# States and scores of a unit in one TensorE block, and where the scores' banks come from

## The chip, the cores and the metric

The kernel runs on one core of one Trainium2 chip. The metric is device time in microseconds (us) of one execution; the reference point is the median of three runs. A core has five engines that work side by side and wait for each other by semaphores: PE (TensorE, matrix products), DVE (VectorE), ACT (ScalarE), POOL (GpSimd) and SP (SyncE, which here only starts transfers). Matrix products write to PSUM, eight banks of 2 KB for each of 128 partitions; VectorE and ScalarE read them from there.

## What is computed

A gated linear recurrence over 768 positions for 4 x 8 heads of width 48, and an MLP with an ELU between its two products on all 3072 tokens:

```python
f = 1.0 / (1.0 + np.exp(-f_logit))
for t in range(S):
    state = f[:, :, t, :, None] * state + np.einsum('bhd,bhe->bhde', k[:, :, t], v[:, :, t])
    y[:, :, t] = np.einsum('bhd,bhde->bhe', q[:, :, t], state)
x = y.transpose(0, 2, 1, 3).reshape(B * S, H * D)          # 3072 x 384
h = x @ w_in                                               # 384 -> 2048
g = np.where(h > 0.0, h, np.exp(np.minimum(h, 0.0)) - 1.0)
out = g @ w_out                                            # 2048 -> 384
```

The weights arrive as 64-bit floats and are unpacked to 32-bit on the chip.

## The kernel before

**Units.** The tokens are cut into 12 units of 256 (u = 0 to 11, three to a sequence, four chunks of 64 in a unit). For a unit the attention part computes, for all 8 heads in 4 pairs: the transposed keys (`transposed`, L669), the products of keys and values that move the state from chunk to chunk (`advance`, L728, tile psU, 64 small matmul records in two banks), the running states (`step`, L686 to L691, one addition a chunk on VectorE; the first of a sequence is a ScalarE copy, L688, the last chunk of a unit that isn't the end of a sequence has a multiplication more, and the last chunk of a sequence has none), the scores within chunks (`scores`, L705, tile psS, 64 records in two banks), the causal mask on them (`mask`, L713, two VectorE instructions, tile at), and then the outputs from the masked scores (`outputs`, L743) and from the states (`carried`, L763, whose results ScalarE copies to xt at L770 and L772, with two transfers after it). The small products use quarters of the array, 64 by 64.

**The MLP** runs one unit behind. It goes in 8 parts P of a unit: `up` (L927 for the first unit, `up7` with L882 for the others, which form the product by seven smaller ones and sums) makes a part of h in tile psH, `joined` (L904) adds the pieces, `exped` (L914, L915) applies the exponential on ScalarE, `elu` (L936) finishes it, POOL forms sums of it (L946), and `down` (L981; L959 for the first unit) accumulates the part into psM, four banks m0 to m3 (m1 and m2 alone for the first unit). After the eighth part `down` has the four banks added and stored (L991, L992). A `down` runs LAG = 2 parts after its `up`.

**Banks.** PSUM's eight banks are two for psH, m0 to m3 for psM, and a0 and a1, which psT, psU, psS and psY of the attention use in turn. A tile that takes a bank waits until the readers of the tile before it are done.

**Order.** The order on each engine is written out by hand: a loop over steps T, 16 to a unit (P = T // 2), with a plan of what else is issued at a step:

```python
if T % 2 and sevens:
    joined(P)
if T % 2 == 0 and P and order[P - 1][0] < DIRECT:
    elu(P - 1)
for f in plan.pop(T, ()):
    f()
if T % 2 == 0:
    up(P)
elif P >= LAG:
    down(P - LAG)
```

An even step ends with an up block and an odd one with a down block on TensorE. The tuples A1, A2 and A3 say at which steps, counted from the unit's first, `attention` issues transposed, advance, step, scores with mask, outputs and carried: for u = 1 at 2, 5, 6, 8, 10, 11, and for u from 3 on at 2, 4, 5, 7, 9, 11 (T in this text is counted from the unit's first step; up(2) is the up block of T=4, "down block 0" the first of the unit whose MLP runs, at T=5). At the steps of u = 1 the weights are still being unpacked: `merge(n)` at step n on VectorE (L581), `split` and `lower` (L563, L567, L573) two steps ahead. There `watch(1)` at step 3 lowers the flag column `fine` (L650) where decays have grown too large. From unit 4 on VectorE also checks the range of the weights again at every fourth step (L603). `warm` (L1036) issues matmuls whose result nobody reads.

Of the kernel before, what the change touches and what calls it, by code (L numbers as in the profile page):

```python
# [356 lines left out]
def fast(ctx: ExitStack, tc: tile.TileContext, q, k, v, f_logit, w_in, w_out, out, flag, outer):  # L357
# [18 lines left out]
    nc = tc.nc  # L376
# [7 lines left out]
    NC = U // C  # L384
    UPB = S // U
    NU = B * UPB
    HP = H // 2
    NFT = DFF // 128
# [5 lines left out]
    LAG = 2  # L394
    AHEAD = 7
    WA = 1
    F1 = (1, 3)
    W0 = 3
    HOLD = 2
    A1 = (2, 5, 6, 8, 10, 11)  # L400
    D2 = (16, 18, 20, 22)
    A2 = (23, 25, 25, 26, 27, 28)
    D3 = (-7, -5, -3, -1)
    A3 = (2, 4, 5, 7, 9, 11)
    BL = 13
    RR = 0
    MX = 10
# [254 lines left out]
    def transposed(u, h, bank, pairs=(0, 1)):  # L662

        if 0 in pairs:
            pts[u, h] = ps.tile([128, 2, NW, 128], FP32, tag=bank, name=f"psT{u}_{h}")
            kns[u, h] = sb.tile([128, 2, NW, 128], FP32, tag="kn", name=f"kn{u}_{h}")
        for p in pairs:
            for w in range(NW):
                nc.tensor.transpose(  # L669
                    pts[u, h][:, p, w], in_=qkf[u % NB]["k"][:, 2 * h + p, w * W : (w + 1) * W], identity=ident[:]  # L670
                )
        p = slice(pairs[0], pairs[-1] + 1)
        nc.scalar.copy(kns[u, h][:, p], pts[u, h][:, p])
# [3 lines left out]
    def step(u, c):  # L677

        if u % UPB == UPB - 1 and c == NC - 1:
            return  # L680
        new = pus[u][c % 2][:, c // 2]
        box = boxes[(u * NC + c) % len(boxes)]
        s = box[:].rearrange("n (p d) -> n p d", d=64)[:, 0:HP, PAD:]
        if u % UPB or c:
            old = sts[u, c][:].rearrange("n (p d) -> n p d", d=64)[:, 0:HP, PAD:]
            nc.vector.tensor_tensor(out=s, in0=new, in1=old, op=ALU.add)  # L686
        else:
            nc.scalar.copy(s, new)  # L688
        if c == NC - 1:
            end = qkf[u % NB]["f"][:, :, 1, U - 1 :].broadcast_to([128, HP, D])  # L690
            nc.vector.tensor_tensor(out=s, in0=s, in1=end, op=ALU.mult)  # L691
        sts[(u, c + 1) if c < NC - 1 else (u + 1, 0)] = box

    def scores(u, banks=("a0", "a1"), pairs=range(HP), pc=None):

        t = qkf[u % NB]
        if pc is None:
            ats[u] = sb.tile([128, 2, NW, HP, C], FP32, tag="at", name=f"at{u}", bufs=1)
            pc = [ps.tile([128, NW, HP, C], FP32, tag=banks[r], name=f"psS{u}_{r}") for r in range(2)]
        for p in pairs:  # L700
            for w in range(NW):
                for b in range(2):
                    cols = slice(w * W + b * C, w * W + b * C + C)
                    for r in range(2):
                        nc.tensor.matmul(  # L705
                            pc[r][FULL[b], w, p], lhsT=t["k"][FULL[r], p, cols], rhs=t["q"][FULL[r], p, cols],
                            start=True, stop=True,
                        )
        return pc

    def mask(u, pc):
        for r in range(2):
            nc.vector.tensor_tensor(  # L713
                out=ats[u][:, r].rearrange("k w p i -> k (w p) i"), in0=pc[r][:].rearrange("k w p i -> k (w p) i"),
                in1=twice[:].unsqueeze(1).broadcast_to([128, NW * HP, C]), op=ALU.mult,
            )

    def advance(u, pairs=range(HP)):

        if u not in pus:  # L720
            pus[u] = [ps.tile([128, NW, HP, D], FP32, tag=n, name=f"psU{u}_{n}") for n in ("a0", "a1")]
        pu = pus[u]
        for p in pairs:
            for w in range(NW):
                for r in range(2):
                    h = 2 * p + r
                    for b in range(2):
                        nc.tensor.matmul(  # L728
                            pu[b][FULL[r], w, p], lhsT=kns[u, p // 2][FULL[b], p % 2, w, FULL[r]],
                            rhs=vs[u % NB][FULL[b], w, PAD + h * D : PAD + (h + 1) * D],  # L730
                            start=(w == 0 and p == 0), stop=(w == NW - 1 and p == HP - 1), skip_group_check=True,
                        )

    def outputs(u, banks=("a0", "a1")):


        pys[u] = [ps.tile([128, NW, HP, C], FP32, tag=banks[b], name=f"psY{u}_{b}") for b in range(2)]
        at = ats.pop(u)
        for w in range(NW):
            for p in range(HP):  # L740
                for r in range(2):
                    for b in range(2):
                        nc.tensor.matmul(  # L743
                            pys[u][b][FULL[r ^ b], w, p], lhsT=of_head(u, b, w, r, p),
                            rhs=at[FULL[b], r, w, p], start=(w == 0 and p == 0), stop=False,
                            skip_group_check=True,
                        )

        for b in range(2):
            nc.scalar.copy(between[:], pys[u][b][:, :, :, 0])  # L750

    def carried(u):

        t = qkf[u % NB]
        py = pys.pop(u)
        for w in range(NW):
            for p in range(HP):
                for b in range(2):
                    c = 2 * w + b
                    if (u % UPB, c) == (0, 0):  # L760
                        continue
                    for r in range(2):
                        nc.tensor.matmul(  # L763
                            py[b][FULL[r ^ b], w, p], lhsT=sts[u, c][FULL[r], 64 * p + r * PAD : 64 * (p + 1) + r * PAD],
                            rhs=t["q"][FULL[r], p, c * C : (c + 1) * C],
                            start=False, stop=True, skip_group_check=True,
                        )
        x = xts[u] = sb.tile([128, HP + 1, U], FP32, tag="xt", name=f"xt{u}", bufs=3)
        to = x[:, 0:HP].rearrange("n p (w b i) -> n b w p i", b=2, i=C)
        nc.scalar.copy(to[:, 0], py[0][:])  # L770
        for r in range(2):
            nc.scalar.copy(to[FULL[r], 1], py[1][FULL[1 - r]])  # L772
        for r in range(2):
            frm = PAD + D * r
            (nc.sync if u > 1 else nc.scalar).dma_start(
                out=x[GAP[r] : GAP[r] + PAD, 0:NKT], in_=x[frm : frm + D, NKT]
            )
# [46 lines left out]
    def at_step(step, *todo):  # L824
        plan.setdefault(step, []).extend(todo)

    def attention(u, first, then):

        kept = []
        for p, i in enumerate(first):  # L830
            at_step(i, (lambda: settle(u)) if p == NKT else lambda p=p: decays(u, p))
        if u > 1:
            at_step(then[0], lambda: transposed(u, 0, "a0"), lambda: transposed(u, 1, "a1"))
        at_step(then[1], lambda: advance(u))
        at_step(then[2], *(lambda c=c: step(u, c) for c in range(NC)))
        at_step(then[3], lambda: kept.append(scores(u)), lambda: mask(u, kept[0]))
        at_step(then[4], lambda: outputs(u))
        at_step(then[5], lambda: carried(u))

    gs, ss, pms, phs = {}, {}, {}, {}  # L840

# [187 lines left out]
        nc.tensor.matmul(pf[0:1, :], lhsT=low[:], rhs=causal[:, W - 1 : W], start=True, stop=True)  # L1029
        nc.vector.tensor_copy(flag[:], pf[0:1, :])  # L1030

    def warm(n, bank="m0"):

        pw = ps.tile([128, 4, 128], FP32, tag=bank, name="psW")
        for _ in range(n):
            nc.tensor.matmul(  # L1036
                pw[:], lhsT=ident[:], rhs=ident[:].unsqueeze(1).broadcast_to([128, 4, 128]), start=True, stop=True
            )
# [81 lines left out]
    at_step(F1[1], lambda: move(1, 1, nc.scalar), lambda: watch(1))  # L1120
    at_step(F1[1] + 2, lambda: scale(1, ("q", NKT, nc.gpsimd)))
    at_step(A1[0], lambda: transposed(1, 0, "a0"), lambda: transposed(1, 1, "a1"))
    attention(1, (), A1)
    at_step(8, lambda: load(2))
    at_step(14, lambda: gates(2))
# [8 lines left out]
    for u in range(3, NU):  # L1134
        t = (u - 1) * NFT
        at_step(t + BL, lambda u=u: blend(u))
        at_step(t - 16, lambda u=u: load(u))
        at_step(t - 8, lambda u=u: gates(u))
        attention(u, [t + i for i in D3], [t + i for i in A3])
    for n in range(NR):  # L1140
        t = 3 * NFT + (NU - 4) * NFT * n // NR + RR
        at_step(t, lambda n=n: reread(n))
# [3 lines left out]
    for T in range(NU * NFT):  # L1146
        P = T // 2
        sevens = order[P][0] >= DIRECT
# [5 lines that stand above are left out]
            f()  # L1154
        if T % 2 == 0:
            up(P)
        elif P >= LAG:
            down(P - LAG)
        for n in later.pop(T, ()):
            split(n)  # L1160
            lower(n)
# [53 lines left out]
```

## Time and profile before

| | us |
|---|---|
| median of three runs | 567.27 (566.85 to 568.79) |
| span of the profiled execution | 567.3 |
| mean granted TensorE clock | 0.997 |
| one unit of TensorE from u = 3 on | 43.7 to 43.8 |

A line of the timeline gives start and length in us, the engine, the line of the kernel, the operation, what it writes and reads, its shape and how many instructions are merged in it; in square brackets is how long the engine stood idle before it and what ended that. PE is TensorE's matmuls and PEld its weight loads. The length of a merged line reaches to the end of its last instruction, and as matmuls overlap, the distance between starts is the better price. The chain of waits follows the end of the kernel back to what released each step.

### The profile page before, as it was taken

The numbers are of one execution on the slowest core, as the hardware profiler recorded it, in microseconds if no ns is written. First come the engines' busy times: TensorE is split into PE (matmuls) and PEld (weight loads), VectorE is DVE, ScalarE is ACT, GpSimd is POOL, SyncE is SP. The second block draws the span as 40 slices with busy tenths as digits, with TensorE's granted clock in tenths as the row PEclk, the third lists the DMA queues.
The fourth block names the chain that finished last, engine by engine and source line by source line (L and its number), as shares of the span: only waits on it lengthen the run. The fifth ranks groups of instructions, "written<-read, shape, count | busy, mean of one in ns | idle before, by whom it ended". The sixth has DMA issues, their size and how long they took to land.

```text
span 567.3 us, 15527 instructions
## 1 busy us (share of the span) xinstructions
PE 547.5 (97%) x6336; PEld 509.7 (90%) x6336; DVE 409.4 (72%) x802; ACT 230.2 (41%) x424; POOL 292.7 (52%) x567
## 2 busy tenths in 40 slices
PE   6879998999999999999999999999999999999996
PEld 3566677999999999999999999999999999999996
DVE  8779989785675785885785885786776876745543
ACT  3287862443343433434343343333343343233331
POOL 6601788475374465456366357257248348325332
PEclk9899999999999999999999999999999999999999
DMA  8997951024024225215216216206206203201001
GB/s 212 266 261 209 298 129 43 3 47 114 3 46 138 65 52 145 79 42 156 78 36 155 86 38 153 86 19 173 84 14 178 84 6 74 84 2 36 29 2 35
DMA packets 38193, 53.30 MB, mean 94 GB/s; under 512 B 3712, under 2 KB 27936, under 8 KB 38112
## 3 DMA queue, kind: packets, MB, share of 16 engines
q1 hardware_dynamic: 37312, 51.62, 34.2%
q8 instruction: 52, 0.85, 0.7%
q10 hardware_dynamic: 800, 0.59, 0.4%
q14 instruction: 29, 0.24, 0.1%
HBM read 44.04 MB, written 4.72 MB: 86 GB/s over the span
## 4 chain that ended last, share of the span: by engine, by line
PE 81%; DMA 7%; DVE 7%; issue 2%; POOL 1%; ACT 1%; SPq 0%; DVEq 0%; ACTq 0%; POOLq 0%
PE psH L882 36%; PE psM L981 36%; DMA area<-in_moe_w_in_dram 4%; PE psS L705 2%; PE psY L743 2%; PE psY L763 2%; PE psU_a L728 2%; DVE f L631 2%; PE psT L669 1%; DMA xt<-xt 1%; DMA f<-f 1%; DVE f L626 1%; DMA k<-in_k_dram 1%; DVE bits L563 1%; DVE area L850 1%
## 5 line engine op out<-in xcount | busy, mean ns | idle before, releaser
L882 PE MATMUL psH<-xt,wi 128*128 128x128 f32 (+1 forms) x1056 | 195.0, 294 | 0.1
L946 POOL TENSOR_TENSOR sums<-gg 128x128 f32<-128x128 f32 x176 | 77.7, 462 | 214.5 <-DVE gg L936 205.9
L882 PEld LDWEIGHTS psH<-xt,wi 128*128 128x128 f32 x1056 | 149.5, 192 | 1.8 <-DVE hh L891 0.4
L914 ACT ACTIVATE gg<-hh 128x512 f32<-128x512 f32 x88 | 55.5, 631 | 232.0 <-DVE hh L904 154.6
L882 PE MATMUL psH<-xt,area 128*128 128x128 f32 x704 | 121.8, 275 | 1.3 <-DVE hh L904 1.0
L882 PEld LDWEIGHTS psH<-xt,area 128*128 128x128 f32 x704 | 106.5, 191 | 6.3 <-PE psH L882 1.3
L891 DVE TENSOR_TENSOR hh<-psH,u 128x256 f32<-128x256 f32 x88 | 37.1, 422 | 93.9 <-ACT u L889 93.9
L981 PE MATMUL psM<-area,sums 128*128 128x192 f32 x528 | 100.2, 326 | 0.0
L981 PEld LDWEIGHTS psM<-area,sums 128*128 128x128 f32 x528 | 88.2, 190 | 0.0
L981 PE MATMUL psM<-wo,gg 128*128 128x192 f32 x352 | 74.9, 335 | 0.0
L631 DVE RECIPROCAL f<-f 128x256 f32<-128x256 f32 x36 | 62.7, 1747 | 1.1
L936 DVE SCALAR_TENSOR_TENSOR gg<-gg,hh 128x512 f32<-128x512 f32 x88 | 61.9, 703 | 1.5 <-ACT gg L915 1.5
L915 ACT ACTIVATE gg<-gg 128x512 f32<-128x512 f32 x96 | 60.6, 631 | 3.0
L981 PEld LDWEIGHTS psM<-wo,gg 128*128 128x128 f32 x352 | 55.2, 190 | 2.0
L904 DVE TENSOR_TENSOR hh<-psH,u43h 128x256 f32<-128x256 f32 (+1 forms) x176 | 54.7, 352 | 3.0
L946 POOL TENSOR_TENSOR sums<-gg,sums 128x128 f32<-128x128 f32 x88 | 47.0, 534 | 6.9
L889 ACT COPY u<-psH 128x128 f32<-128x128 f32 x88 | 23.1, 263 | 60.9 <-PE psH L882 60.9
L621 POOL TENSOR_TENSOR q<-q,f 128x256 f32<-128x256 f32 x48 | 35.7, 745 | 21.8 <-DVE f L631 10.6
L904 DVE TENSOR_TENSOR u43h<-psH,hh 128x256 f32<-128x256 f32 x88 | 37.1, 422 | 12.7 <-PE psH L882 12.4
L621 POOL TENSOR_TENSOR k<-k,f 128x256 f32<-128x256 f32 x48 | 40.7, 851 | 7.1 <-DMA f<-f 5.1
L981 PE MATMUL psM<-area,gg 128*128 128x192 f32 x176 | 43.0, 326 | 0.0
L981 PE MATMUL psM<-wo,sums 128*128 128x192 f32 x176 | 43.0, 326 | 0.0
(97 smaller groups left out, 672.3 us busy)
## 6 DMA issues: line engine op xcount, KB each, us to landing
area<-in_moe_w_out_dram SPq DMA_DIRECT2D x8, 768.0 KB, 9.6
again<-in_moe_w_in_dram SPq DMA_DIRECT2D x16, 384.0 KB, 4.2
again<-in_moe_w_out_dram SPq DMA_DIRECT2D x16, 384.0 KB, 3.5
k<-in_k_dram SPq DMA_DIRECT2D x12, 384.0 KB, 4.5
q<-in_q_dram SPq DMA_DIRECT2D x12, 384.0 KB, 5.4
v<-in_v_dram SPq DMA_DIRECT2D x12, 384.0 KB, 5.8
area<-in_moe_w_in_dram SPq DMA_DIRECT2D x8, 576.0 KB, 8.4
out_dram<-o SPq DMA_DIRECT2D x42, 96.0 KB, 1.7
```

Source lines behind the costliest of these rows:

```text
L621: e.tensor_tensor(out=t[n][:, p], in0=t[n][:, p], in1=t["f"][:, p, "kq".index(n)], op=ALU.mult)
L631: nc.vector.reciprocal(f[:, p, 1], f[:, p, 0])
L705: nc.tensor.matmul(pc[r][FULL[b], w, p], lhsT=t["k"][FULL[r], p, cols], rhs=t["q"][FULL[r], p, cols], start=True, stop=True,)
L882: nc.tensor.matmul(to, lhsT=lhs, rhs=rhs, start=(n == 0), stop=True, skip_group_check=True)
L889: nc.scalar.copy(u1[:], pa[:, 0])
L891: add = lambda to, x, y: nc.vector.tensor_tensor(out=to, in0=x, in1=y, op=ALU.add)
L904: add = lambda to, x, y: nc.vector.tensor_tensor(out=to, in0=x, in1=y, op=ALU.add)
L914: nc.scalar.activation(g[:], h, AF.Relu, scale=-1.0)
L915: nc.scalar.activation(g[:], g[:], AF.Exp, scale=-1.0)
L936: nc.vector.scalar_tensor_tensor(out=g[:], in0=g[:], scalar=-1.0, in1=phs.pop(P), op0=ALU.add, op1=ALU.max)
L946: nc.gpsimd.tensor_tensor(out=s[:, i], in0=x, in1=y, op=op)
L981: nc.tensor.matmul(pm[bank][:, half * DH : (half + 1) * DH], lhsT=x, rhs=y, start=first, stop=(j == NP - 1), skip_group_check=True,)
```

## The change

A function `both` issues, at one step, the state products in a0 and a1, the scores in m3 and m0, the state additions and the masks. It takes the place of three entries of `attention` where the tuple has four steps instead of six. This holds for u = 1 (steps 2, 6, 8, 10) and for u = 3 to 7 and 9 to 11 (2, 5, 9, 11); u = 2 and u = 8 (`APART`) stay as they were. For the later units the down block of the step with `both` is left out and issued two steps later, ahead of the one that stands there, since m0 and m3 are psM's. For u = 1 the MLP of the first unit uses m1 and m2 alone, and no down block moves. At step 4 of u = 1, 31 matmuls of one column by one column are issued in m3, reading `fine`.

```diff
+    SMALL = 31
-    A1 = (2, 5, 6, 8, 10, 11)
+    A1 = (2, 6, 8, 10)
-    A3 = (2, 4, 5, 7, 9, 11)
+    A3 = (2, 5, 9, 11)
+    APART, B3 = 8, (2, 4, 5, 7, 9, 11)
...
+    def both(u):
+        advance(u)
+        pc = scores(u, ("m3", "m0"))
+        for c in range(NC):
+            step(u, c)
+        mask(u, pc)
...
-        at_step(then[1], lambda: advance(u))
-        at_step(then[2], *(lambda c=c: step(u, c) for c in range(NC)))
-        at_step(then[3], lambda: kept.append(scores(u)), lambda: mask(u, kept[0]))
-        at_step(then[4], lambda: outputs(u))
-        at_step(then[5], lambda: carried(u))
+        if len(then) == 4:
+            at_step(then[1], lambda: both(u))
+        else:
+            at_step(then[1], lambda: advance(u))
+            at_step(then[2], *(lambda c=c: step(u, c) for c in range(NC)))
+            at_step(then[3], lambda: kept.append(scores(u)), lambda: mask(u, kept[0]))
+        at_step(then[-2], lambda: outputs(u))
+        at_step(then[-1], lambda: carried(u))
...
-    def warm(n, bank="m0"):
+    def warm(n, bank="m0", small=0):
         pw = ps.tile([128, 4, 128], FP32, tag=bank, name="psW")
+        for _ in range(small):
+            nc.tensor.matmul(pw[0:1, 0, 0:1], lhsT=fine[:, 0], rhs=fine[:, 0], start=True, stop=True)
...
+    at_step(4, lambda: warm(0, "m3", SMALL))
...
-        attention(u, [t + i for i in D3], [t + i for i in A3])
+        attention(u, [t + i for i in D3], [t + i for i in (B3 if u == APART else A3)])
+    joint = [(u - 1) * NFT + A3[1] for u in range(3, NU) if u != APART]
...
-        elif P >= LAG:
+        elif P >= LAG and T not in joint:
+            if T - 2 in joint:
+                down(P - LAG - 1)
             down(P - LAG)
```

## The prediction

> **What bounds the kernel now.** I read the page first: busy shares, then the chain of waits. TensorE is busy for 97% of the span, and from about 100 us on the chain is nothing but its blocks in turn.
>
> ```profile
> PE 547.5 (97%) x6336; PEld 509.7 (90%) x6336; DVE 409.4 (72%) x802; ACT 230.2 (41%) x424; POOL 292.7 (52%) x567
> ```
>
> So an edit gains only what it takes out of TensorE's own stream, and loses what it makes TensorE wait. I then read the timeline of one unit by engine (the eighth, u = 7; columns are start, length, engine, line, operation, count). TensorE:
>
> ```profile
> 310.50 0.49 PE L981 MATMUL psM<-wo,sums 128*128 128x192 f32 x2
> 310.92 1.15 PE L728 MATMUL psU_a<-v,kn 64*64 64x48 f32 x64
> 312.00 0.49 PE L882 MATMUL psH<-xt,wi 128*128 128x128 f32 x2
> ...
> 314.55 0.82 PE L981 MATMUL psM<-wo,gg 128*128 128x192 f32 x4
> ...
> 319.36 1.16 PE L705 MATMUL psS<-q,k 64*64 64x64 f32 x64
> 320.45 0.92 PE L981 MATMUL psM<-wo,gg 128*128 128x192 f32 x4
> ```
>
> Here T=4 is the state block (310.92) and the up block, 314.55 is the first down block of the new unit (T=5), 319.36 the scores (T=7). Starts give the prices. An up block is 2.44 us and a down block 2.28 where neither touches attention (chain of waits). An attention block of 64 records takes 1.09 (319.36 to 320.45), 17 ns a record; around it the last matmul before and the first ones after are stretched by 0.09 and 0.10, so it costs 1.28. Now VectorE in the same unit:
>
> ```profile
> 311.46 0.36 DVE L991 TENSOR_TENSOR o<-psM,u 128x192 f32<-128x192 f32 x1 [1.62 <-ACT u L992]
> ...
> 315.56 0.42 DVE L904 TENSOR_TENSOR u43h<-psH,hh 128x256 f32<-128x256 f32 x1
> 316.01 0.62 DVE L904 TENSOR_TENSOR hh<-psH,u43h 128x256 f32<-128x256 f32 x2
> 316.55 1.52 DVE L686 TENSOR_TENSOR state<-psU_a,state 128x192 f32<-128x192 f32 x4
> 318.11 0.36 DVE L691 TENSOR_TENSOR state<-state,f 128x192 f32<-128x192 f32 x1
> ...
> 320.57 1.29 DVE L713 TENSOR_TENSOR at<-psS,twice 128x512 f32<-128x512 f32 x2
> ```
>
> The reader is to see that VectorE is on average free but here is not: from 311.46 (output additions of the unit before) to the end of the state additions at 318.39 it never idles. The state block was done near 312.1 and its additions start at 316.55, over 4 us later; the kernel before hides that because the masks (320.57) come two steps later and nobody waits for them until T=9. In units that begin a sequence it is later still (u = 9):
>
> ```profile
> 405.42 0.30 ACT L688 COPY state<-psU_a 128x192 f32<-128x192 f32 x1
> ```
>
> That copy stands behind the activations of T=5 on ScalarE, and VectorE idles 1.63 us for it until 405.75. Last, the start, where the weights are unpacked:
>
> ```profile
> 38.69 2.83 PE L927 MATMUL psH<-xt,wi 128*128 128x256 f32 x12 [2.30 <-DVE wi L581]
> ```
> ```profile
> 42.18 0.10 DVE L650 SCALAR_TENSOR_TENSOR fine<-f,fine 128x3 f32<-128x3 f32 x1
> ```
> ```profile
> 550.16 0.19 PE L1029 MATMUL psF<-causal,low 128*1 128x1 f32 x2
> ```
>
> TensorE starts up(2) (T=4) at 38.69; the flag column `fine` is written at 42.18 by T=3's work, as VectorE is behind; and a one-column matmul's two records start 0.19 - 0.164 = 0.026 us apart.
>
> **What the Trainium skill says.** "TensorEngine Tiling (Array Packing)", Key Properties: changing the tiling mode drains the array. The trace agrees: 0.19 us per 64x64 block. "TensorE: Matmul & The Clock Gate", table at the head: VectorE is a strict first-in first-out queue, and Part 3: matmuls start in program order. The trace agrees (every block in the order of the program), so a mask can't pass the state additions, and no later matmul can pass a waiting one. Same page, Part 1: the array falls to half clock after an idle window of some 3.4 us. Before, 2.30 us of idling at 36.4 to 38.69 left the granted clock at 1.00; the opening matmuls of 512 columns took 0.82 to 0.86 us each cold against 0.46 later.
>
> **The change, part by part.**
>
> *Merging the two blocks, units 3 to 7 and 9 to 11.* 64 + 64 records are the same; one entry and one exit go: -0.19 us in each of 8 units, -1.5.
>
> *Down block 0 moved from T=5 to T=7.* 14 records, same length, no DMA. It is the first to write banks m0 and m3, which the scores now hold until both masks have read them. Queued behind it on TensorE is everything. Its arrival: up(2) now starts at the old state block's start less 0.09, then 2.44 + 0.09 + 128 x 0.017 = 2.18 + 2.44 + 0.10 = 7.25 us. For u = 7: 310.83 + 7.25 = 318.08. The masks: VectorE's chain is set by the output additions, which do not move, so state additions still end at 318.39, then 1.29 of masks: 319.68, and 0.12 for the release (a state addition ended at 51.85 and the score load that needed its bank began at 51.97). TensorE goes on at 319.80: it stands 1.72 us. The same subtraction elsewhere:
> - u = 4, 7, 10 (four additions and a multiplication): 1.7 each, 5.2 in all.
> - u = 5, 11 (three additions; for u = 11 they end at 492.77, masks 494.05, release 494.17, arrival 485.89 + 7.25 = 493.14): 1.0 each, 2.1.
> - u = 6, 9 (ScalarE copy first; u = 9: end 407.20, masks 408.49, release 408.61, arrival 398.32 + 7.25 = 405.57): 3.0 each, 6.1; u = 3, without the 1.0 us of range checks at T=4: end 143.77, release 145.17, arrival 143.03: 2.1.
>
> Together 15.4 us. A smaller wait of some 0.2 (the second half of up(3) on the bank that `joined` reads until 316.63) lies inside it. Nothing gives it back: from there TensorE is the bound, and down blocks 0 and 1 run back to back in the same total. The products and sums that wait longer for block 0 have four and three buffers; the third sum at T=8 needs the one that block 0 frees at T=7, which is in time. Net of the drains: +13.9.
>
> *Second unit, small matmuls at T=4.* They read `fine`, which the watch at T=3 writes: TensorE stands from 36.4 to about 42.4, not 38.69. 31 x 2 records by 0.026 are 1.6 us, with 0.1 for the change of mode (bounds: 0.017 a record as in the attention blocks, 1.1 us; 0.164, no overlap at all, 10.2 us; the pair that the trace shows is nearest). up(2) starts at 44.1, 5.4 later than before.
>
> *Second unit, block at T=6, outputs at 8, carried at 10.* From up(2) to the 17th step TensorE has 6 up blocks of 2.63, 6 down blocks of 2.62, and attention of 2.37 + 1.28 + 1.28: 36.4 us, so that step starts at 80.5 against 77.67: +2.8. Before, the stretch took 38.98, of which 36.6 was work by the same prices and 2.4 waits (at 45.3, 51.5, 52.0, 63.4); I let these all go, since TensorE now comes late, and 0.2 is the drain saved. VectorE is delayed by the activation of up(2), by 1.2 to 3.7 us, but stays ahead (the fused block's additions and masks end near 54.5 and outputs come at 57.2; the wi merge for up(7) ends near 72.1, wanted at 75.4). The move of carried brings three xt copies of 1.75 us on ScalarE and two DMA issues on its queue ahead of the activation of up(5); `blend` then still ends near 77.6.
>
> *Clock.* Six idle us may drop the clock. Cost: none if no idle window falls in the gap; at most about 4 us (small matmuls and up(2) at half rate). I take 1.5. Second unit in all: +4.3.
>
> Sum on the profiled run's 567.3 us (its span; the median of three runs is 567.27, so nothing lies around it to add): 567.3 + 13.9 + 4.3 = 585.5.
>
> **The rivals.**
> 1. The second unit's delay is swallowed: this stretch is paced by unpacking on VectorE and ScalarE and TensorE's 5.4 us vanish in it. For: VectorE idles little from 39.65 to 69. Against: TensorE waited only 2.4 us there. Early +0.5, time 581.7.
> 2. The clock drops after the 3 us stops too. For: they come near the idle window. Against: they are under it. Three units (3, 6, 9) by 2 us more: 591.5.
> 3. Other side: the masks are done when down block 0 arrives, so the new blocks only lose drains. Its place is bank m0 at T=7; it decides if VectorE's chain ends 1.0 us (u = 5, 11) to 3.0 us (u = 6, 9) earlier than read, and if `fine` is no wait. Then -1.7 for nine units and -1.5 for waits before scores and carried in the second: 564.1. For: VectorE's total of 72% leaves room. Against: the chain at 311.46 to 318.39 has no gap and is fed by output additions that don't move.
> 4. Masks in time, but `fine` waited for: 567.3 - 1.5 + 4.3 = 570.1.
>
> **How the numbers follow.** Forecast 585.5: chance 0.63. Rival 1: 0.15; rival 2: 0.09; rival 3: 0.07; rival 4: 0.06. The likeliest alone: 582 to 589 (small matmuls and clock -2.5 to +2.5; release lag and overlap of VectorE's instructions by 0.2 in 8 units). To hold 8 in 10 the range takes in rival 1 and most of rival 2: 579 to 591. Below 0.3% (1.7 us) a measurement can't be told from no change. Faster by more than that: rival 3 less its weak form, 0.06; within it: 0.02; slower: 0.92.
>
> **What would show it.** Right: in the timeline a first psM block of each of the eight units that starts 7.25 + 1 to 3 us after the up block of T=4, with TensorE idle before it and VectorE's `at` (L713's successor) as releaser, about 15 us in all, in three sizes by position in the sequence; 128 small records in one run of about 2.2 us; one idle stretch of near 6 us ending with `fine`, then 62 records 0.026 apart; T=16 about 3 to 4 us later. Wrong: down block 0 follows without a gap, or the gap is alike in all units (then the state copy and the additions aren't what sets it), or up(2) starts near 39. Faster than 567 would mean that VectorE's masks were early, and the reading of its chain fails.

## The result, and the profile after

The changed kernel takes 588.33 us (median of six runs, 585.31 to 590.18) against 567.96 for the kernel before (six runs too; the first three had a median of 567.27): 1.0354 times as long, 95% interval 1.0325 to 1.0382. The profiled execution has a span of 584.5 us and took 586.35. The median lies inside the forecast range of 579 to 591, 2.8 us above the forecast of 585.5. That forecast was summed on a span, from the first instruction to the last, and in every run that lists both, the time is 1.7 to 1.9 us longer than the span; so the profile's span of 584.5, 1.0 below it, is the like comparison.

The busy line of the changed kernel, from its page: TensorE works nearly as long as before (547.5), but in a longer span.

```profile
PE 549.0 (94%) x6398; PEld 511.4 (87%) x6398; DVE 409.0 (70%) x802; ACT 230.4 (39%) x424; POOL 291.2 (50%) x567
```

Who waited for whom, changed kernel (total us, times, longest). These are the largest of TensorE's new waits: eight on the masks, one on the flag. L994 is `down` here, L715 the mask, L1049 the small matmuls and L652 the flag (lines of the kernel before stand 2 to 13 further down here).

```profile
PE psM L994 <- DVE at L715: 11.6, 8, 2.5
...
PE psW L1049 <- DVE fine L652: 6.0, 1, 6.0
```

TensorE's timeline in the eighth unit (u = 7), to be laid beside the one shown before:

```profile
320.82 0.38 PE L895 MATMUL psH<-xt,wi 128*128 128x128 f32 x2
...
323.36 1.15 PE L730 MATMUL psU_a<-v,kn 64*64 64x48 f32 x64
324.33 1.14 PE L707 MATMUL psS<-q,k 64*64 64x64 f32 x64
325.39 0.49 PE L895 MATMUL psH<-xt,wi 128*128 128x128 f32 x2
...
326.79 0.68 PE L895 MATMUL psH<-xt,area 128*128 128x128 f32 x4 [0.23 <-DVE hh L917]
...
329.80 0.92 PE L994 MATMUL psM<-wo,gg 128*128 128x192 f32 x4 [1.23 <-DVE at L715]
```

and VectorE's there:

```profile
326.01 0.62 DVE L917 TENSOR_TENSOR hh<-psH,u43h 128x256 f32<-128x256 f32 x2
326.55 1.59 DVE L688 TENSOR_TENSOR state<-psU_a,state 128x192 f32<-128x192 f32 x4
328.18 0.36 DVE L693 TENSOR_TENSOR state<-state,f 128x192 f32<-128x192 f32 x1
328.46 1.28 DVE L715 TENSOR_TENSOR at<-psS,twice 128x512 f32<-128x512 f32 x2
```

The masks end at 329.74 and down block 0 starts at 329.80. From the start of up(2) to that block it is 8.98 us (329.80 - 320.82). The other seven units by the same subtraction: 9.31 for u = 3, 8.97 for u = 4 and 10, 8.18 and 8.19 for u = 5 and 11, 10.23 and 10.22 for u = 6 and 9. The figure in brackets (1.23 here, 11.6 in all) is less than what a stop costs, as it counts only from the end of the matmul before, and leaves out the shorter stop inside up(3) at 326.79; distances between starts hold both.

The start, TensorE:

```profile
41.13 1.69 PE L1049 MATMUL psW<-fine 128*1 128x1 f32 x62 [5.96 <-DVE fine L652]
42.75 5.02 PE L940 MATMUL psH<-xt,wi 128*128 128x256 f32 x12
47.61 2.74 PE L972 MATMUL psM<-wo,gg 128*128 128x384 f32 x8
```

TensorE stands 5.96 us for the flag. The granted clock is the share of full speed at which TensorE was let run. up(2) then takes 4.86 us from start to start where it took 2.76 before; the table of stretches (length, then busy us of each engine, then the granted clock, the DMA share and GB/s) has the reason in the clock column:

```profile
43.00:45.00 2.00, 2.00 (x5) 1.59 (x6) 1.93 (x4) 1.49 (x1) 0.00 (x0) 0.50 1.11 207
```

Profiles begin the second unit up to some 2 us apart (its transposes start at 32.76 before, at 31.55 in the changed kernel). So I cut each in two: from the start of the second unit's transposes to the up block of step 16, and from there to the end of the span. These two columns are of one profiled execution each; the medians are of all executions.

| kernel | transposes to step 16 | step 16 to the end | median us | times before (95%) |
|---|---|---|---|---|
| before | 44.91 | 489.63 | 567.96 | |
| changed | 49.29 | 503.66 | 588.33 | 1.0354 (1.0325 to 1.0382) |
| masks first | 50.23 | 489.46 | 572.26 | 1.0073 (1.0048 to 1.0098) |
| no small matmuls | 48.36 | 503.35 | 584.63 | 1.0329 (1.0258 to 1.0399) |
| second unit only | 48.73 | 489.56 | 572.35 | 1.0086 (1.0059 to 1.0112) |
| later units only | 44.66 | 505.16 | 584.50 | 1.0296 (1.0270 to 1.0321) |
| small ones, no flag | 49.66 | 504.73 | 587.04 (one run) | |
| nine fillers | 48.96 | 504.11 | 588.46 | 1.0353 (1.0318 to 1.0387) |
| six fillers | 47.22 | 506.46 | 587.54 | 1.0339 (1.0300 to 1.0378) |
| masks first, checks moved, old second unit | 45.07 | 486.57 | 565.29 | 0.9948 (0.9930 to 0.9965) |
| the same, second unit fused at step 8 | 45.14 | 487.00 | 565.48 | 0.9945 (0.9927 to 0.9962) |

The changed kernel loses 4.4 us in the first part and 14.0 in the second, 18.4 in all; between the medians it is 20.4.

### The profile page after: what moved, and what is told of

It is laid out like the page before. It is cut to its first block, busy times and chain, and to the rows that moved or that the text cites. A ratio compares the mean times of both kernels' runs of the same rounds, so it can differ in the third digit from the quotient of the medians.

```text
span 584.5 us, 15648 instructions
## 1 busy us (share of the span) xinstructions
PE 549.0 (94%) x6398; PEld 511.4 (87%) x6398; DVE 409.0 (70%) x802; ACT 230.4 (39%) x424; POOL 291.2 (50%) x567
## 4 chain that ended last, share of the span: by engine, by line
PE 85%; DVE 8%; issue 2%; DMA 2%; POOL 1%; ACT 1%; ACTq 0%; DVEq 0%; POOLq 0%
PE psM L994 35%; PE psH L895 32%; PE psM L972 3%; PE psH L940 3%; PE psY L745 2%; PE psY L765 2%; PE psS L707 2%; PE psU_a L730 2%; DVE at L715 2%; DVE state L688 2%; PE psT L671 1%; DVE f L633 1%; DMA f<-f 1%; DVE hh L917 1%; DMA k<-in_k_dram 1%
## 5 line engine op out<-in xcount | busy, mean ns | idle before, releaser
L994 PE MATMUL psM<-area,sums 128*128 128x192 f32 x528 | 100.2, 326 | 0.0
L994 PEld LDWEIGHTS psM<-area,sums 128*128 128x128 f32 x528 | 88.2, 190 | 0.0
L994 PE MATMUL psM<-wo,gg 128*128 128x192 f32 x352 | 74.8, 335 | 11.6 <-DVE at L715 11.6
L994 PEld LDWEIGHTS psM<-wo,gg 128*128 128x128 f32 x352 | 55.6, 190 | 14.5 <-DVE at L715 13.1
L994 PE MATMUL psM<-area,gg 128*128 128x192 f32 x176 | 43.0, 326 | 0.0
L994 PE MATMUL psM<-wo,sums 128*128 128x192 f32 x176 | 43.0, 326 | 0.0
```

What stands on the lines that cost most here:

```text
L994: nc.tensor.matmul(pm[bank][:, half * DH : (half + 1) * DH], lhsT=x, rhs=y, start=first, stop=(j == NP - 1), skip_group_check=True,)
```

## The experiments

My theory: in the later units TensorE stops at down block 0 for masks that stand behind the state additions on VectorE; in the second unit it stops for the flag, at a falling clock. The rivals: the stops belong to the moved down blocks or their banks as such, or come from the second unit's delay; and the small matmuls keep a clock that would fall without them.

**Masks first** (on the changed kernel).

```diff
         pc = scores(u, ("m3", "m0"))
+        mask(u, pc)
         for c in range(NC):
             step(u, c)
-        mask(u, pc)
```

> The masks are issued ahead of the state additions in the fused step; nothing else differs from the changed kernel. Theory (down block 0 waits for masks that stand behind the state additions on VectorE): masks now follow the additions of T=5 at once and end at or before TensorE's arrival, so the stops of 0.8 to 2.9 us before the first psM block of eight units vanish, down block 0 follows up(3) within 0.1 us in all of them, and some 14 us go: about 571 to 573 us, 1.008 times the kernel before. Rival (the stop belongs to the pair of down blocks or to banks m0 and m3, whoever reads them): time stays within 2 us of the changed kernel's.

Measured: 572.26 us, and the second part is back at 489.46 (the first is 0.9 us longer than the changed kernel's; 0.4 of it is up(2), which took 5.28 us at half clock). VectorE in u = 7 of this run:

```profile
319.24 0.62 DVE L917 TENSOR_TENSOR hh<-psH,u43h 128x256 f32<-128x256 f32 x2
319.78 1.28 DVE L715 TENSOR_TENSOR at<-psS,twice 128x512 f32<-128x512 f32 x2
320.97 1.52 DVE L688 TENSOR_TENSOR state<-psU_a,state 128x192 f32<-128x192 f32 x4
```

TensorE there:

```profile
318.62 0.49 PE L895 MATMUL psH<-xt,wi 128*128 128x128 f32 x2
...
320.01 0.68 PE L895 MATMUL psH<-xt,area 128*128 128x128 f32 x4 [0.23 <-DVE hh L917]
...
321.63 0.82 PE L994 MATMUL psM<-wo,gg 128*128 128x192 f32 x4
```

The masks end at 321.06, and the psM block at 321.63 has no idle time before it. The moved down blocks and the banks m0 and m3 are as in the changed kernel; the order of five to seven VectorE instructions alone takes the 14 us away, and with them all eight stops at down block 0. The rival that the stops belong to the pair or the banks falls. What is left is the stop inside up(3) at 320.01, for the addition that `joined` ends at 319.86: up(3) takes 3.01 us here where it takes 2.54 without it.

**Later units only**: `A1 = (2, 5, 6, 8, 10, 11)` and no `at_step(4, ...)`. **Second unit only**: A3 with six steps again.

```diff
-    A3 = (2, 5, 9, 11)
+    A3 = (2, 4, 5, 7, 9, 11)
...
-    joint = [(u - 1) * NFT + A3[1] for u in range(3, NU) if u != APART]
+    joint = []
```

> The second unit as in the kernel before and no small matmuls; units from 3 on as in the changed kernel. Theory: 14 us over the kernel before, with the same eight stops in three sizes (0.8, 1.9 and 2.2 to 3.1 us). Rival (stops come from the second unit's delay): under 4 us over.

> Units from 3 on as in the kernel before; the second unit and the small matmuls as in the changed kernel. Theory (sum of two independent parts): 4.4 us over the kernel before (3 to 6.5 by where the clock's window falls), no stops at the first psM blocks. Rival (the second unit's delay is what shifts the later units' VectorE work): more than 10 us over.

Measured: 16.6 us over the kernel before (584.50 - 567.93, the median of before in that batch) and 4.4 (572.35 - 567.93). The eight stops are there without the second unit's change (11.6 us in total, the figure of the changed kernel) and absent with it alone. So the parts are independent, and their sum of 21.0 stands against 20.4 for both together. The first came out 2.6 above expectation; its profile, 15.3 over by the two parts, has one reason in it: after the stop of u = 9 the granted clock was 0.59 and 0.56 for two stretches of 2 us, and from that unit's state block to the next it took 48.28 us instead of the changed kernel's 46.62.

**No small matmuls** (the line at step 4 left out) and **small matmuls that don't read the flag**:

```diff
-            nc.tensor.matmul(pw[0:1, 0, 0:1], lhsT=fine[:, 0], rhs=fine[:, 0], start=True, stop=True)
+            nc.tensor.matmul(pw[0:1, 0, 0:1], lhsT=ident[:, 0:1], rhs=ident[:, 0:1], start=True, stop=True)
```

> The 31 small matmuls at step 4 are left out of the changed kernel; the rest stays. Theory (they make TensorE wait for the flag, and the clock drops in the 6 us): up(2) starts as soon as its weights are merged, near 38 us, and takes 2.7 instead of 4.9; the fused block then waits some 4 us for the last scaled q, so that only about 3.4 us of the 4.4 come back: 581 to 583 in a profile like the one of 584.5. Rival (they keep TensorE's clock up over a gap that is there anyway): no faster than the changed kernel, and up(2) slow here too.

> The 31 small matmuls of the changed kernel read a column of the identity instead of the flag column. Theory (the wait for the flag delays up(2), not the matmuls themselves): 62 records stand in the gap from 36 to 38 us, up(2) starts near 38 as without them, and the fused block waits near 4 us for the scaled q; up to step 16 it is like the run without small matmuls, some 1 us ahead of the changed kernel. Rival (the small matmuls cost by themselves): up(2) is late by their 1.6 us.

Without them, TensorE:

```profile
37.02 2.83 PE L940 MATMUL psH<-xt,wi 128*128 128x256 f32 x12 [2.30 <-DVE wi L583]
...
48.89 0.51 PE L707 MATMUL psS<-q,k 64*64 64x64 f32 x16 [3.83 <-POOL q L623]
49.33 4.44 PE L940 MATMUL psH<-xt,wi 128*128 128x256 f32 x12
```

up(2) is early and fast, as expected, and the fused block then stands for the last scaled q, 3.83 us for its last 16 records; that multiplication waits on POOL for a transfer. Of the 3.4 us that I expected back in the first part only 0.9 came (49.29 to 48.36). Counted from the transposes, up(3) starts 2.5 us earlier than in the changed kernel; then the clock fell in this wait too, and up(3) took 4.28 us from start to start instead of 2.70. The time of the whole run, 584.63 us (583.44 to 591.31), doesn't decide between theory and rival, as its interval overlaps with the changed kernel's; the timeline does: up(2) is not slow. With small matmuls on the identity (one execution, so I read only its timeline), up(2) starts at 36.85, 5.94 after the transposes, against 5.93 without any: the flag alone made it late. But up(2) took 4.35 us there and up(3) 5.28, and the first part was no shorter (49.66), against the expectation of a gain of 1 us. This speaks against the rival that small matmuls keep the clock: 62 of them in the gap did not, and it was 0.72 on average from 36 to 40.

**Fillers**: matmuls of 512 columns on the identity ahead of the small ones, nine and then six.

```diff
-    at_step(4, lambda: warm(0, "m3", SMALL))
+    at_step(4, lambda: warm(9, "m3"), lambda: warm(0, "m3", SMALL))
```

> Nine matmuls of 512 columns on the identity, some 4 us, are issued ahead of the small ones in the changed kernel, so that TensorE idles under 2 us before the flag. Theory (the clock falls to half in the 6 us): the granted clock stays 1.00, up(2) takes 2.7 instead of 4.9, and step 16 comes 2.2 us earlier: 2 us off the changed kernel. Rival (up(2) is slow because its weights or tokens come late): up(2) stays near 4.9.

Measured: no gain. Each filler is two records, so nine of them ran from 35.20 to 43.1, 1.9 past the flag. The clock did stay at 1.00 and up(2) took 2.69 us, but it started 1.8 us later. The size was wrong, so I ran it again with six:

> Six filling matmuls in place of nine ahead of the small ones: 12 records of 0.437 us, as the run with nine showed 18 of them in 7.9 us, so that they end near 40.5 and the flag, not the fill, releases the small ones. Theory (half clock makes up(2) slow): the granted clock stays 1.00, the small matmuls start with the flag near 41.3 as in the changed kernel, up(2) takes 2.7, and step 16 comes 2.2 us earlier than in the changed kernel (47.1 us after the transposes instead of 49.3). Rival (something else delays step 16): up(2) short, but step 16 still 49 us after the transposes.

TensorE in the run with six:

```profile
34.99 5.31 PE L1051 MATMUL psW<-ident 128*128 128x512 f32 x12
41.20 1.69 PE L1049 MATMUL psW<-fine 128*1 128x1 f32 x62 [0.90 <-DVE fine L652]
42.82 2.86 PE L940 MATMUL psH<-xt,wi 128*128 128x256 f32 x12
```

up(2) takes 2.69 us, and step 16 comes 47.22 us after the transposes: 2.07 of the second unit's 4.4 us were the clock. So up(2) was slow by the clock, and the rival falls. The whole run is not clearly faster (587.54, with overlapping intervals), and in its profile the second part is 2.8 us longer. The stops of u = 6 and u = 9 show why: after each, the way to the next unit's state block is 1.67 us longer than in the changed kernel. The stop of u = 6 has the changed kernel's length, 2.48 us, but here the matmuls after it are slow, and the clock stands at 0.50 from 284 to 286:

```profile
281.99 0.92 PE L994 MATMUL psM<-wo,gg 128*128 128x192 f32 x4 [2.48 <-DVE at L715]
282.75 1.45 PE L994 MATMUL psM<-area,sums 128*128 128x192 f32 x6
283.99 0.84 PE L994 MATMUL psM<-area,gg 128*128 128x192 f32 x2
```

```profile
284.00:286.00 2.00, 2.00 (x8) 2.00 (x8) 0.78 (x2) 1.94 (x3) 0.74 (x2) 0.50 0.00 0
```

In the changed kernel's profile the third of these matmul lines took 0.49 us after the same stop.

**A version that beats both.** Masks first, the ninth unit fused too, the old second unit without small matmuls (A1 as before), and the range checks one step later, so that they stand behind the masks and not ahead of `joined`. The lines that no run above has:

```diff
-        at_step(t + 4, lambda n=n: check(n))
+        at_step(t + 5, lambda n=n: check(n))
...
-    APART, B3 = 8, (2, 4, 5, 7, 9, 11)
+    APART, B3 = -1, (2, 4, 5, 7, 9, 11)
```

> Masks ahead of the state additions, the ninth unit fused too, the range checks moved from the even step to the odd one after it (behind the masks), the second unit as in the kernel before and no small matmuls. Theory: the eight stops go, and the 0.47 us that up(3) still loses on VectorE in seven units goes with the check; what stays is the drain and the shorter block, 0.33 us in nine units: 3.0 us under the kernel before, 0.995. Rival (VectorE's tail moves the loss on to outputs or to the next up block): no faster than the kernel before.

> As the run beside it (masks ahead, checks moved, nine later units fused, no small matmuls), and the second unit fused too, but at step 8 where its scores stood before, with outputs at 10 and carried at 11. Theory (the second unit's loss comes from the block standing at step 6, before its scaled q is there): the wait for q is gone, step 16 comes no later than in the kernel before and up to 1 us earlier: 3 to 4 us under the kernel before, 0.993 to 0.995. Rival (fusing itself costs there): slower than the run beside it by 1 us or more.

Measured: 565.29 us, 0.9948 times the kernel before (0.9930 to 0.9965), and 565.48 with the second unit fused at step 8. The first of the two, TensorE in u = 7:

```profile
307.60 0.38 PE L895 MATMUL psH<-xt,wi 128*128 128x128 f32 x2
...
312.17 0.49 PE L895 MATMUL psH<-xt,wi 128*128 128x128 f32 x2
...
314.71 0.82 PE L994 MATMUL psM<-wo,gg 128*128 128x192 f32 x4
```

From up(2) to down block 0 it is 7.11 us with no idle time. Two up blocks and two separate attention blocks took 2 x 2.44 + 2 x 1.28 = 7.44, so fusing saves 0.33 us a unit, 3.0 in nine; the second part fell by 3.06. Moving the checks and fusing the ninth unit were not run one by one. Fusing at step 8 ended the wait for q (the block has none there), which supports that standing at step 6 was the fault. It gained nothing that can be told apart, as the intervals of the two versions overlap; in its profile up(2) fell to half clock (4.22 us to the next block), and whether it did so in the other executions no trace shows.

## Why the prediction was right

- *The base of the sum.* The prediction took the span of 567.3 us and the median time of 567.27 for one quantity, and saw "nothing" that "lies around it to add". That they agree is chance: spans here are 1.7 to 1.9 us shorter than their times. The difference is free of this: 18.2 us forecast, 18.4 in the two parts of the profiles, 20.4 between the medians.
- *Stops at down block 0.* Right in place, cause and size. Forecast from up(2) to down block 0 were 7.25 plus the stop: 8.97, 8.28, 10.29 and 9.39 for the four kinds of units. Measured: 8.98, 8.19, 10.22 and 9.31. That the masks' end and not the arrival sets this is why it came out so near.
- *Drains.* Mis-sized: 0.19 us a unit was forecast, 0.33 measured. I took the two blocks of 64 at 17 ns a record inside the fused block too. There psU's records go at 15 ns (323.36 to 324.33 for 64), and the scores after them at the 17 ns of a lone block (324.33 to 325.39), so that 0.12 of the 0.14 lie in the first 64. Against the true arrival at 7.11 the stops are 16.2 us in all (2.20 + 3 x 1.87 + 2 x 1.08 + 2 x 3.12), not 15.4; less 8 x 0.33 that is 13.6. The two errors cancel, as both come from the arrival that was set 0.14 us late while the end of the masks decides; so the near total does not confirm the price of the drains. The 13.9 of the forecast stand against 14.0 in the second part; the 0.4 between 13.6 and 14.0 I did not follow up.
- *Wait for the flag and the small matmuls.* Right: 6.0 us of standing forecast, 5.96 measured; 1.6 us for 62 records, 1.62 measured.
- *Clock.* Mis-sized: 1.5 us forecast as a mean over chance. It fell in all three profiles that stood the whole 6 us at that place: up(2) took 4.86 us there, 5.28 with masks first and 4.30 with the second unit only, against 2.69 behind the fillers. That is 2.2 in the changed kernel and 1.6 to 2.6 over the three.
- *The second unit as a whole.* 4.3 us forecast, 4.4 measured, but put down to the flag and the clock behind it alone. The prediction's faster rival counted 1.5 us of gain if the flag were no wait. That is wrong: without the flag the block at step 6 comes before its scaled q and stands 3.83 us for it, and 3.4 of the 4.4 us remain in that profile, 1.6 of them by the clock. In the kernel before, that multiplication ends on POOL at 49.35; the prediction does not mention it, and so does not ask what a TensorE that comes early would meet.
- *Rivals.* The first (early delay swallowed) falls: it stayed whole. The second, a clock that drops after the stops too, was held for a case apart and is probably a part of the result: it happens in some executions (in the profile of later units only after u = 9, with six fillers after u = 6 and 9), not in the changed kernel's profile. Executions of the changed kernel with a mean clock of 0.993 took 585.3 and 586.4 us, and those with 0.981 took 590.1 and 590.2. So such drops can account for what lies between forecast and median; the longer executions have no trace that would show where theirs fell. The Trainium skill, "TensorE: Matmul & The Clock Gate", Part 1, has an idle window of some 3.4 us for the drop; here 2.48 us of standing were enough in 4 cases of 12, so the measurement decides: I should have let it in below that length. The third and the fourth, masks in time, fall for the change as made; masks first showed what it takes.

## What to carry to other kernels

When a block is moved onto a bank that another phase needs next, ask not how long the engine that frees the bank works but what stands ahead of the freeing instruction in its queue: two masks of 1.3 us make TensorE stop for 1 to 3 us a unit behind the state additions, and not at all at that place ahead of them. An average of 72% busy says nothing about an engine's lag at one point; take it from the timeline, with the start of the chain that feeds it. And a matmul put in to fill a gap waits for its operand like any other: choose one that nobody writes.

## What the runs showed of the hardware

- The granted clock fell to half after waits of 2.3 to 2.5 us in some executions and not in others. After 2.30 us of idling up(2) took 2.7 us in four profiles and 4.2 in one, with the same TensorE program up to there; of twelve stops of 2.48 us at down block 0 (u = 6 and 9 in six profiles) four were followed by half clock. One execution can't rule such a drop out.
- Where the wait falls goes with this. Between the opening and the last 5 us, the eleven profiles have twelve spells at half clock; in stretches of 0.2 us, each lasts 3.41 us, 6.83 or 10.24, that is one, two or three times 3.41. Where an execution has several, they start whole multiples of 3.41 us apart (283.44 and 419.98 with six fillers: 40 times). I laid a grid of 3.41 us through each profile. In the stretch of the grid ahead of ten of the twelve drops TensorE had stood 1.96 us or more, and in those without a drop 1.97 at most; the other two drops followed small matmuls. So in these profiles a stop of 2.48 us dropped the clock when some 2.0 of it fell into one stretch, and the grid lies otherwise in each execution. A drop cost 1.67 us, about half of its 3.41, where TensorE had work all through it (48.29 us against 46.62 for the unit of u = 6).
- Small matmuls, 62 records in 1.62 us, did not hold the clock: in the one execution with them on the identity, after them and 0.69 us of idling, it was at half for most of up(2).
- In a fused block of 128 quarter-array records the first 64 go at 15 ns each (0.97 us), against 17 when 64 stand alone (1.09); the trace shows the difference, not its cause.
